# Dilated and windowed attention with expert adapters: masks and scores moved to all four 64x64 tiles of the TensorE array, row ends and last token chunks made full-array products

## The chip, the cores and the metric

The kernel runs on one core of a Trainium2 chip. The metric is device time in microseconds (us); lower is better. Engines are named as in the profile: PE is TensorE (matmul), PEld its weight loads, DVE is VectorE, ACT is ScalarE, POOL is GpSimd, SP issues some of the transfers. Matmul ends are modelled in the trace, so this text measures TensorE by the starts of its instructions wherever it can.

"Slow" is here a run over 1.5% above the fastest of the same kernel in its set. The kernel before had two groups of times on each of the three chips of the experiments, 119.3 to 120.8 us and 121.8 to 123.7 us. Comparisons below use fast runs. Chips also differ, by up to 2.2 us for the changed kernel, so kernels are compared within one call, which ran on one chip. Each mean is of two to four fast runs.

## The reference, cut to what matters

```python
# q, k, v: (8 batches, 8 heads, 576 positions, 64)
scores = q @ k.T / sqrt(64)
# heads 0-3: 0 <= rel < 32;   heads 4-7: 0 <= rel < 128 and rel % 4 == 0
attn = softmax(where(mask, scores, -1e9))
x = (attn @ v) as (8*576 tokens, 512)
logits = x @ w_gate                      # 8 experts, two chosen
out = x + sum over chosen e of w_e * (x @ A[e]) @ B[e]     # rank 16
```

## The kernel before

Positions of the dilated heads are reordered by residue, so every mask is a band. A score unit handles two heads of one batch ("hp" 0 to 3, so four units a batch). The 576 keys make nine blocks of 64; each block needs the scores of at most 96 queries. The masks are written to PSUM first, as a product with an identity, and the scores are added on top.

```python
def scores(b, hp):
    t = kqt(b, hp)                       # head a on partitions 64a .. 64a+63
    for k in range(2):                   # two PSUM banks: key blocks 0-4 and 5-8
        rows = slice(64 * k, 64 * k + 64)
        ...
        nc.tensor.matmul(banks[k][:, 0 : n * SEG], lhsT=two[rows], rhs=mask, start=True, ...)   # 64 x 128 tile
    for j in range(NB):
        k, c = divmod(j, 5)
        for a in range(2):
            rows = slice(64 * a, 64 * a + 64)
            nc.tensor.matmul(banks[k][rows, SEG * c : SEG * c + n],                               # 64 x 64 tile
                lhsT=t[rows, 0, 64 * j : 64 * j + 64], rhs=t[rows, 1, 64 * j : 64 * j + n], ...)
```

Only two of the four 64x64 tiles are used, the two that lie straight: head 0 goes from partitions 0-63 to 0-63, head 1 from 64-127 to 64-127.

Then follow the exponential (ACT, line 309), the products with the values (PE, lines 329 and 340), the division by the row sum (DVE, 351 and 352), a cast (POOL, 363), transposes (PE, 371), the gates (PE, 403), the routing (DVE, 424 to 444), the weighting (POOL, 449), transposes of the weighted hidden values (PE, 462), the expert outputs (PE, 486 and 498) and the final sums (DVE, 508 and 515). 576 tokens are four chunks of 128 and one of 64; the chunk of 64 takes part-array products:

```python
# end of the rows, in values():  64 columns of P: a 128 x 64 tile per head
nc.tensor.matmul(o[64 * h : 64 * h + 64, 260:390]..., lhsT=p[:, at : at + 64], rhs=bdv(b, hp, j), ...)
# gates():  m = 64 for the last chunk
nc.tensor.matmul(g[0:m, ...], lhsT=xt[:, k, 128 * c : 128 * c + m], rhs=AW[:, k], ...)
# gturn():  m = 64 for the last chunk
nc.tensor.transpose(tp[:, 128 * c : 128 * c + m], gz[0:m, c], ident[0:m, 0:m])
```

A small list scheduler in the kernel fixes the order of every engine's instructions in advance, from planned costs ("S" 620 ns, and so on). Engines then run in that order.

The softmax here doesn't subtract the row's maximum and nothing guards it: scores larger than these inputs give would overflow.

## Time and profile before

| | |
|---|---|
| time, median of 2 runs | 123.06 us |
| time / span of the profiled run, of the lower group | 120.8 / 119.0 us |
| last load lands | 75.0 us |
| last scores unit starts / last values product starts | 88.0 / 95.1 us |
| PE share of the chain of waits | 60% |

The first fence has lines of the kernel before's page: busy time of each engine, then busy tenths and the granted TensorE clock in 40 slices of 3 us, then the chain that ended last by engine (the work followed back from the last instruction, at each step to what released it).

```profile
PE 92.2 (77%) x1496; PEld 69.2 (58%) x1496; DVE 75.2 (63%) x220; ACT 70.4 (59%) x155; POOL 59.4 (50%) x86
...
PE   0105979999999999999999989999999915910540
...
DVE  6870536346578748996967759877986880193360
...
PEclk9999999999999999999999999999999997695555
...
PE 60%; DMA 13%; DVE 8%; POOL 8%; issue 5%; POOLq 1%; ACT 1%; DVEq 0%; ACTq 0%
```

PE stands at 9 in nearly every slice from 21 to 95 us, and the chain runs on PE for 60% of the span. Utilization alone would not prove the limit; the chain says that the work that ended last was, for that long, waiting for PE alone.

The second fence is the kernel before's timeline of PE: start, duration, line, what, tile rows*columns, output shape, count.

```profile
62.50 0.37 PE L290 MATMUL bs<-cb 64*128 64x480 bf16 x2
62.80 0.56 PE L298 MATMUL bs<-slot 64*64 64x96 bf16 x18
63.29 0.37 PE L290 MATMUL bs<-cb 64*128 64x480 bf16 x2
63.59 0.56 PE L298 MATMUL bs<-slot 64*64 64x96 bf16 x18
64.08 0.37 PE L290 MATMUL bs<-cb 64*128 64x480 bf16 x2
64.39 0.56 PE L298 MATMUL bs<-slot 64*64 64x96 bf16 x18
64.88 0.64 PE L329 MATMUL bs<-slot,p 128*128 128x130 bf16 x8
```

Read the starts, not the durations (which include latency): 62.50, 63.29, 64.08 are units 0.79 us apart. From mask to score is 0.30 us although 480 columns stream in 0.20 at the full clock: the other 0.10 goes where the tile shape changes. It changes again at the end of every unit. The single starts inside a unit are below (not a view of the profile; read from the trace's records, in us).

```
63.290 63.293 | 63.593 63.597 | 63.660 63.663 | 63.704 63.708 | 63.746 63.749 | ... | 63.959 63.963 | next unit 64.083
 2 masks        9 pairs of scores, 0.041 to 0.044 apart (0.067 after the first); then 0.120 to the next mask
```

### The profile page before, as it was taken

What the parts mean: (1) busy time and instruction counts of PE and PEld (TensorE: products, weight loads), DVE (VectorE), ACT (ScalarE), POOL (GpSimd) and SP (SyncE); (2) the same over time, 40 slices, a digit from 0 to 9 for tenths busy, and PEclk for the clock granted to TensorE, in tenths of its full rate; (3) what the DMA queues carried; (4) which work ended last, traced back from release to release, by engine and by line L of the source; (5) the groups of instructions that cost most, each with busy time, mean ns of one, the idle gap of its engine ahead of it and who ended that gap; (6) DMA issues with size and microseconds to landing.
All of it is one profiled execution on the core that took longest, in us unless ns stands there. A gap on an engine that the chain in (4) does not pass through costs nothing.

```text
span 119.0 us, 3669 instructions
## 1 busy us (share of the span) xinstructions
PE 92.2 (77%) x1496; PEld 69.2 (58%) x1496; DVE 75.2 (63%) x220; ACT 70.4 (59%) x155; POOL 59.4 (50%) x86
## 2 busy tenths in 40 slices
PE   0105979999999999999999989999999915910540
PEld 0005747777677778867787768787768704700210
DVE  6870536346578748996967759877986880193360
ACT  7927445868666868657776786668478633300200
POOL 6805172661798299259933850546266415404400
PEclk9999999999999999999999999999999997695555
DMA  3999999999999999999999999998640053009054
GB/s 102 223 212 219 208 217 218 208 215 213 215 211 220 210 213 217 211 215 213 218 210 216 215 216 353 427 424 378 274 195 6 0 248 149 0 0 396 0 219 178
DMA packets 4864, 24.64 MB, mean 207 GB/s; under 512 B 752, under 2 KB 1136, under 8 KB 3952
## 3 DMA queue, kind: packets, MB, share of 16 engines
q0 software_dynamic: 2848, 14.23, 58.9%
q1 hardware_dynamic: 2000, 10.19, 21.1%
q8 instruction: 11, 0.18, 0.6%
q14 instruction: 5, 0.04, 0.1%
HBM read 29.21 MB, written 9.44 MB: 325 GB/s over the span
## 4 chain that ended last, share of the span: by engine, by line
PE 60%; DMA 13%; DVE 8%; POOL 8%; issue 5%; POOLq 1%; ACT 1%; DVEq 0%; ACTq 0%
PE bs L329 14%; DMA slot<-in_kv_dram 13%; PE bs L298 12%; PE bs L403 10%; PE bs L371 6%; PE bs L290 6%; PE bs L486 5%; DVE x L508 3%; POOL slot L232 3%; PE bs L462 2%; PE bs L340 2%; POOL gz L449 2%; DVE x L352 1%; POOLq L636 1%; POOL gn L472 1%
## 5 line engine op out<-in xcount | busy, mean ns | idle before, releaser
L363 POOL CAST xb<-x 128x512 bf16<-128x512 f32 (+1 forms) x32 | 21.3, 671 | 30.7 <-DVE sm L444 15.3
L309 ACT ACTIVATE p<-bs 128x480 bf16<-128x480 f32 x64 | 30.9, 538 | 9.0 <-PE bs L298 7.8
L329 PE MATMUL bs<-slot,p 128*128 128x130 bf16 x352 | 27.4, 224 | 1.0 <-ACT p L309 1.0
L352 DVE TENSOR_TENSOR x<-bs,rc 128x384 f32<-128x384 f32 x48 | 26.8, 557 | 1.6
L508 DVE TENSOR_TENSOR x<-x,bs 128x512 f32<-128x512 f32 x32 | 20.2, 682 | 11.6 <-PE bs L486 11.4
L329 PEld LDWEIGHTS <-p 128*128 128x128 bf16 x352 | 21.8, 98 | 2.7 <-ACT p L309 1.7
L351 DVE RECIPROCAL rc<-bs 128x6 f32<-128x6 f32 x48 | 9.2, 191 | 22.2 <-PE bs L329 21.1
L298 PE MATMUL bs<-slot 64*64 64x96 bf16 (+1 forms) x576 | 18.8, 208 | 5.6 <-DMA slot<-in_kq_dram 5.4
L298 PEld LDWEIGHTS <-slot 64*64 64x64 bf16 x576 | 14.7, 109 | 13.3 <-issue 6.8
L232 POOL DMA_DIRECT2D slot<-in_kv_dram x32 | 16.7, 532 | 7.3 <-DMA slot<-in_kq_dram 4.7
L371 PE MATMUL bs<-cb,xb 128*128 128x128 bf16 x144 | 13.3, 220 | 3.9 <-POOL xb L363 3.9
L290 PE MATMUL bs<-cb 64*128 64x480 bf16 (+1 forms) x64 | 12.8, 363 | 3.4 <-DMA cb<-in_cb_dram 3.4
L449 POOL TENSOR_TENSOR gz<-zs,sm 128x640 bf16<-128x640 f32 x8 | 10.2, 1274 | 9.7 <-DVE sm L444 9.6
L472 POOL COPY gn<-gd 128x576 bf16<-128x576 bf16 x8 | 11.8, 1475 | 4.8 <-ACT gd L467 4.8
L391 ACT COPY xt<-bs 128x512 bf16<-128x512 bf16 x16 | 9.4, 587 | 6.5 <-PE bs L371 6.2
L403 PE MATMUL bs<-aw,xt 128*128 128x136 bf16 (+1 forms) x160 | 13.1, 236 | 0.0
L371 PEld LDWEIGHTS <-xb 128*128 128x128 bf16 x144 | 8.6, 97 | 5.8 <-POOL xb L363 4.3
L381 ACT COPY xt<-bs 128x512 bf16<-128x512 bf16 x16 | 9.4, 591 | 4.2 <-PE bs L371 4.1
L403 PEld LDWEIGHTS <-xt 128*128 128x128 bf16 (+1 forms) x160 | 10.7, 106 | 1.5 <-issue 0.2
L413 ACT COPY zs<-bs 128x408 f32<-128x408 f32 (+1 forms) x16 | 6.9, 443 | 5.4 <-PE bs L403 3.8
L462 PE MATMUL bs<-cb,gz 128*128 128x128 bf16 (+1 forms) x40 | 4.7, 235 | 6.4 <-POOL gz L449 6.2
L467 ACT ACTIVATE gd<-bs 128x576 bf16<-128x576 bf16 x8 | 5.2, 653 | 5.2 <-PE bs L462 4.3
(36 smaller groups left out, 75.4 us busy)
## 6 DMA issues: line engine op xcount, KB each, us to landing
slot<-in_kv_dram POOLq DMA_DIRECT2D x30, 434.2 KB, 13.9
out_dram<-x SPq DMA_DIRECT2D x7, 1152.0 KB, 6.9
out_dram<-x SPq DMA_DIRECT2D x2, 512.0 KB, 2.6
slot<-in_kq_dram POOLq DMA_DIRECT2D x2, 288.0 KB, 8.7
slot<-in_kv_dram POOLq DMA_DIRECT2D x2, 146.2 KB, 8.5
x<-in_aw_dram SPq DMA_DIRECT2D x1, 272.0 KB, 2.8
x<-in_bt_dram SPq DMA_DIRECT2D x1, 256.0 KB, 7.9
cb<-in_cb_dram SPq DMA_DIRECT2D x1, 208.0 KB, 2.6
```

Source lines behind the costliest of these rows:

```text
L232: insts[name] = nc.gpsimd.dma_start(out=dst, in_=src)
L290: nc.tensor.matmul(banks[k][:, 0 : n * SEG], lhsT=two[rows], rhs=mask, start=True, stop=False, skip_group_check=True)
L298: nc.tensor.matmul(banks[k][rows, SEG * c : SEG * c + n], lhsT=t[rows, 0, 64 * j : 64 * j + 64], rhs=t[rows, 1, 64 * j : 64 * j + n], star ...
L309: nc.scalar.activation(buf(("P", b, hp), P)[:, 5 * k : 5 * k + n, 0:SEG], buf(("S", b, hp), BS, k)[:, 0 : n * SEG].rearrange("p (j c) -> p ...
L329: nc.tensor.matmul(o[:, 130 * r : 130 * r + 130].rearrange("p (a d) -> p a d", a=2), lhsT=p[:, at : at + 128], rhs=bdv(b, hp, j), start=(n ...
L352: nc.vector.tensor_tensor(X[b][:, st, 3 * k : 3 * k + 3].rearrange("p r (a d) -> p r a d", a=2), o[:, :, :, 0:D], rc.unsqueeze(3).to_broad ...
L363: nc.gpsimd.tensor_copy(buf(("xb", b, hp), XB)[:, 0:n], X[b][:, st, 4 * h : 4 * h + n])
L371: nc.tensor.transpose(tp[:, 128 * u : 128 * u + 128], xb[:, u], ident)
L403: nc.tensor.matmul(g[0:m, GW * n : GW * n + GW], lhsT=xt[:, k, 128 * c : 128 * c + m], rhs=AW[:, k], start=(k == 0), stop=(k == 3), skip_g ...
L449: nc.gpsimd.tensor_tensor(buf(("gz", b), GZ).rearrange("p c (e r) -> p c e r", e=E), buf(("zs", b), ZS)[:, :, 0:ER].rearrange("p c (e r) - ...
L472: nc.gpsimd.tensor_copy(buf(("g", b), GN).rearrange("p (i c) -> p c i", c=C), buf(("g", b), GD).rearrange("p (c i) -> p c i", c=C),)
L508: nc.vector.tensor_tensor(x, x, d.rearrange("p (u h c) -> p u h c", u=2, h=2), ALU.add)
```

## The change

The intent is to run masks and scores on all four 64x64 tiles, so that the tile shape does not change inside a unit and four products run abreast, and to turn the 64-token leftovers into full-array products, so that the shape does not change there either. For the second half of the key blocks (bank 1), head 0 is sent to partitions 64-127 and head 1 to 0-63. The Trainium skill, "PSUM — Partial Sum Buffer", section "PSUM bank collisions raise a hardware error", says that row tiles may not write one bank and the same partitions at once; with the swap each bank is filled by two row tiles on different partitions. The values of those blocks are swapped on the host side of the layout to match.

```diff
 def scores(b, hp):
             for k in range(2):
-                rows = slice(64 * k, 64 * k + 64)
-                nc.tensor.matmul(banks[k][:, 0 : n * SEG], lhsT=two[rows], rhs=mask, start=True, ...)
+                for a in range(2):
+                    rows = slice(64 * a, 64 * a + 64)
+                    to = slice(64 * (a ^ k), 64 * (a ^ k) + 64)
+                    nc.tensor.matmul(banks[k][to, 0:n], lhsT=ident[rows, rows], rhs=CB[rows, at : at + n], start=True, ...)
-            for j in range(NB):
+            jobs = [(j, j, 64 * j, min(SEG, S - 64 * j)) for j in range(NB)]
+            if hp % 2:
+                jobs.append((9, 7, 512, 32))          # scores again, for the row end as a full-array product
+            for seg, j, q, n in sorted(jobs, key=lambda x: x[0] % 5):      # alternates the banks
                 ...
-                        banks[k][rows, ...]
+                        banks[k][to, ...]
 def values(b, st, k):     # end of the rows
-                        o[64 * h : 64 * h + 64, 260:390]..., lhsT=p[:, at : at + 64]      # 2 per head
+                    o[:, 260:390]..., lhsT=p[:, at : at + 128]                            # 4 accumulated
 def gates(b, part):
-                m = min(128, S - 128 * c)
+                at = min(128 * c, S - 128)            # last chunk overlaps the one before
 def gturn(b):  same, gz[:, c] whole
 # removed: setting parts of PSUM to zero at the start (pinit)
 # constants in SBUF: 832 -> 2048 columns (208 -> 512 KB)
 # planned costs: scores 620 -> 600 with 140 for a change of tile shape; others to what a trace showed
```

The cuts leave out the scheduler's new "mode" and the tables of constants. The issue order is planned anew, so it differs too.

More of the change, by code (lines that the diff above doesn't have):

```diff
@@ L45, in constants, with __init__ @@
     eye = np.eye(128, dtype=np.float32)
-    two = np.tile(np.eye(64, dtype=np.float32), (2, 2))
-    plain = np.tile(band(()), (2, 1))
-    dil = np.zeros((128, 5 * SEG), np.float32)
-    for j in range(NB):
-        m = band([e - 64 * j for e in (I, 2 * I, 3 * I)])
-        r, c = (0, j) if j < 5 else (64, j - 5)
-        dil[r : r + 64, c * SEG : (c + 1) * SEG] = m
-    return np.concatenate([eye, two, plain, dil], 1).astype(ml_dtypes.bfloat16)
+    none = np.full((64, SEG), NEG, np.float32)
+    last = np.where(np.arange(SEG) < 64, band(()), NEG)
+    spill = np.concatenate([band(())[:, 64:], none[:, 32:]], 1)
+    plain = [band(())] * 8 + [last, spill]
+    dil = [band([e - 64 * j for e in (I, 2 * I, 3 * I)]) for j in range(8)] + [last, spill]
+    m = np.concatenate(plain + dil, 1)
+    return np.concatenate([eye, np.concatenate([m, m], 0)], 1).astype(ml_dtypes.bfloat16)
 class Op:
-    def __init__(self, name, eng, dur, deps, prio, emit, alloc=(), free=(), lat=120):
+    def __init__(self, name, eng, dur, deps, prio, emit, alloc=(), free=(), lat=120, mode=0):
+        self.mode = mode
         self.name, self.eng, self.dur, self.deps = name, eng, dur, deps
@@ L68, in __init__, with add @@
         self.held = {}
-    def add(self, name, eng, dur, deps, prio, emit, alloc=(), free=(), lat=120):
-        op = Op(name, eng, dur, deps, prio, emit, alloc, free, lat)
+    def add(self, name, eng, dur, deps, prio, emit, alloc=(), free=(), lat=120, mode=0):
+        op = Op(name, eng, dur, deps, prio, emit, alloc, free, lat, mode)
         assert name not in self.ops, name
@@ L81, in order @@
         clock = {}
+        mode = 0
         todo = list(self.ops.values())
@@ L95, in order @@
                 t = clock.get(o.eng, 0.0)
+                if o.eng == "PE" and o.mode != mode:
+                    t += 140
                 for d in o.deps:
@@ L116, in order @@
             clock[o.eng] = o.end
+            mode = o.mode if o.eng == "PE" else mode
             for pool, key, n in o.alloc:
@@ L155, in attn_adapters_kernel @@
     X = [one.tile([128, 2, NB, 128], FP, name=f"x{b}") for b in range(B)]
-    P = [one.tile([128, NB, PER], BF, name=f"p{i}") for i in range(NP)]
+    P = [one.tile([128, NB + 1, PER], BF, name=f"p{i}") for i in range(NP)]
     XB = [one.tile([128, 5, 128], BF, name=f"xb{i}") for i in range(4)]
@@ L164, in attn_adapters_kernel @@
     RC = [one.tile([128, 3, 2], FP, name=f"rc{i}") for i in range(4)]
-    CB = one.tile([128, 256 + 6 * SEG], BF, name="cb")
+    CB = one.tile([128, 128 + 20 * SEG], BF, name="cb")
     AW = one.tile([128, 4, GW], BF, name="aw")
@@ L170, in attn_adapters_kernel @@
     ident = CB[:, 0:128]
-    two = CB[:, 128:256]
-    mplain = CB[:, 256 : 256 + SEG]
-    mdil = CB[:, 256 + SEG : 256 + 6 * SEG]
     stage = X[B - 1].rearrange("p s n c -> p (s n c)")
@@ L200, in pzeros @@
         return emit
-    def pinit():
-        for t in BS:
-            nc.vector.memset(t[64:128, GW : 2 * GW], 0.0)
     def first(name, fn, dur, nbytes):
@@ L211, in first @@
         add(name, "HQ", nbytes / 430.0, [name + "_i"], -1, emit, lat=900)
-    first("cb", lambda: nc.sync.dma_start(out=CB, in_=cb), 0, 128 * 832 * 2)
+    first("cb", lambda: nc.sync.dma_start(out=CB, in_=cb), 0, 128 * 2048 * 2)
     first("awf", lambda: nc.sync.dma_start(out=awf, in_=aw), 0, 128 * 544 * 4)
@@ L262, in attn_adapters_kernel @@
         add(f"pz{i}", "DVE", 520, [], -4 + i, pzeros(i))
-    add("pinit", "DVE", 900, [], -5, pinit)
     def kqt(b, hp):
@@ L276, in bdv, with segs @@
         ap = [list(x) for x in base.ap]
-        return bass.AP(base.tensor, base.offset, [ap[0], [V1, 2], [1, 65]])
+        if j < 5:
+            return bass.AP(base.tensor, base.offset, [ap[0], [V1, 2], [1, 65]])
+        return bass.AP(base.tensor, base.offset + V1, [ap[0], [-V1, 2], [1, 65]])
+    def segs(hp, k):
+        return 4 if k and hp % 2 == 0 else 5
     def scores(b, hp):
@@ L283, in emit @@
             for k in range(2):
-                rows = slice(64 * k, 64 * k + 64)
-                n = 5 - k
-                if hp < 2:
-                    mask = mplain[rows].unsqueeze(1).to_broadcast([64, n, SEG])
-                else:
-                    mask = mdil[rows, 0 : n * SEG]
-                nc.tensor.matmul(
-                    banks[k][:, 0 : n * SEG], lhsT=two[rows], rhs=mask, start=True, stop=False, skip_group_check=True
-                )
-            for j in range(NB):
-                k, c = divmod(j, 5)
-                n = min(SEG, S - 64 * j)
+                n = segs(hp, k) * SEG
+                at = 128 + 10 * SEG * (hp // 2) + 5 * SEG * k
                 for a in range(2):
                     rows = slice(64 * a, 64 * a + 64)
+                    to = slice(64 * (a ^ k), 64 * (a ^ k) + 64)
                     nc.tensor.matmul(
-                        banks[k][rows, SEG * c : SEG * c + n],
+                        banks[k][to, 0:n], lhsT=ident[rows, rows], rhs=CB[rows, at : at + n],
+                        start=True, stop=False, skip_group_check=True,
+                    )
+            jobs = [(j, j, 64 * j, min(SEG, S - 64 * j)) for j in range(NB)]
+            if hp % 2:
+                jobs.append((9, 7, 512, 32))
+            for seg, j, q, n in sorted(jobs, key=lambda x: x[0] % 5):
+                k, c = divmod(seg, 5)
+                for a in range(2):
+                    rows = slice(64 * a, 64 * a + 64)
+                    to = slice(64 * (a ^ k), 64 * (a ^ k) + 64)
+                    nc.tensor.matmul(
+                        banks[k][to, SEG * c : SEG * c + n],
                         lhsT=t[rows, 0, 64 * j : 64 * j + 64],
-                        rhs=t[rows, 1, 64 * j : 64 * j + n],
+                        rhs=t[rows, 1, q : q + n],
                         start=False, stop=True, skip_group_check=True,
@@ L307, in emit @@
         def emit():
-            n = 5 - k
+            n = segs(hp, k)
             nc.scalar.activation(
@@ L335, in emit @@
                 return
-            for h in range(2):
-                hp = 2 * st + h
-                p = buf(("P", b, hp), P).rearrange("p j c -> p (j c)")
-                for n, (at, j) in enumerate([(8 * PER, 8), (7 * PER + 64, 7)]):
-                    nc.tensor.matmul(
-                        o[64 * h : 64 * h + 64, 260:390].rearrange("p (a d) -> p a d", a=2),
-                        lhsT=p[:, at : at + 64], rhs=bdv(b, hp, j),
-                        start=(n == 0), stop=(n == 1), skip_group_check=True,
-                    )
+            jobs = [(0, 8 * PER, 8), (0, 7 * PER + 64, 7), (1, 8 * PER - 64, 8), (1, 9 * PER - 64, 7)]
+            for n, (h, at, j) in enumerate(jobs):
+                p = buf(("P", b, 2 * st + h), P).rearrange("p j c -> p (j c)")
+                nc.tensor.matmul(
+                    o[:, 260:390].rearrange("p (a d) -> p a d", a=2),
+                    lhsT=p[:, at : at + 128], rhs=bdv(b, 2 * st + h, j),
+                    start=(n == 0), stop=(n == 3), skip_group_check=True,
+                )
         return emit
@@ L400, in emit @@
             for n, c in enumerate(range(3) if part == 0 else range(3, 5)):
-                m = min(128, S - 128 * c)
+                at = min(128 * c, S - 128)
                 for k in range(4):
                     nc.tensor.matmul(
-                        g[0:m, GW * n : GW * n + GW], lhsT=xt[:, k, 128 * c : 128 * c + m], rhs=AW[:, k],
+                        g[:, GW * n : GW * n + GW], lhsT=xt[:, k, at : at + 128], rhs=AW[:, k],
                         start=(k == 0), stop=(k == 3), skip_group_check=True,
@@ L460, in emit @@
             for c in range(5):
-                m = min(128, S - 128 * c)
-                nc.tensor.transpose(tp[:, 128 * c : 128 * c + m], gz[0:m, c], ident[0:m, 0:m])
+                at = min(128 * c, S - 128)
+                nc.tensor.transpose(tp[:, at : at + 128], gz[:, c], ident)
         return emit
@@ L534, in attn_adapters_kernel @@
             t = t0 + hp * T / 4
-            add(f"S{b}{hp}", "PE", 620, loaded(b, st, h, "k") + ["cb", "pinit"], t, scores(b, hp), alloc=[("s", ("S", b, hp), 2)], lat=200)
+            add(f"S{b}{hp}", "PE", 600, loaded(b, st, h, "k") + ["cb"], t, scores(b, hp), alloc=[("s", ("S", b, hp), 2)], lat=200, mode=1)
             add(f"E{b}{hp}0", "ACT", 580, [f"S{b}{hp}"], t, exps(b, hp, 0), alloc=[("p", ("P", b, hp), 1)], free=[("S", b, hp)], lat=150)
-            add(f"E{b}{hp}1", "ACT", 490, [f"S{b}{hp}", f"E{b}{hp}0"], t, exps(b, hp, 1), free=[("S", b, hp)], lat=150)
+            add(f"E{b}{hp}1", "ACT", 580 if h else 490, [f"S{b}{hp}", f"E{b}{hp}0"], t, exps(b, hp, 1), free=[("S", b, hp)], lat=150)
             if h == 0:
@@ L550, in attn_adapters_kernel @@
                 fr = [("P", b, 2 * st)] + ([("P", b, hp)] if k else [])
-                add(f"V{b}{st}{k}", "PE", (440, 440, 530)[k], deps, t + 1.5 + k / 10, values(b, st, k),
+                add(f"V{b}{st}{k}", "PE", (470, 470, 580)[k], deps, t + 1.5 + k / 10, values(b, st, k),
                     alloc=[("s", ("O", b, st, k), 1)], free=fr, lat=200)
@@ L562, in attn_adapters_kernel @@
         for part in range(2):
-            add(f"G{b}{part}", "PE", 780 if part == 0 else 500, [f"U{b}{hp}" for hp in range(4)] + ["aw"], t, gates(b, part),
+            add(f"G{b}{part}", "PE", 710 if part == 0 else 480, [f"U{b}{hp}" for hp in range(4)] + ["aw"], t, gates(b, part),
                 alloc=[("s", ("G", b, part), 1)], free=[("xt", b)], lat=200)
@@ L570, in attn_adapters_kernel @@
         add(f"W{b}", "DVE", 195, [f"H{b}"], t + 2, weigh(b))
-        add(f"Y{b}", "POOL", 1500, [f"W{b}"], t + 2.5, gated(b), alloc=[("gz", ("gz", b), 1)], free=[("zs", b)])
+        add(f"Y{b}", "POOL", 1280, [f"W{b}"], t + 2.5, gated(b), alloc=[("gz", ("gz", b), 1)], free=[("zs", b)])
         add(f"K{b}", "PE", 300, [f"Y{b}"], t + 4, gturn(b), alloc=[("s", ("GT", b), 1)], free=[("gz", b)], lat=200)
         add(f"J{b}", "ACT", 650, [f"K{b}"], t + 4, gcopy(b), alloc=[("g", ("g", b), 1)], free=[("GT", b)])
-        add(f"M{b}", "POOL", 680, [f"J{b}"], t + 4.5, gnat(b))
+        add(f"M{b}", "POOL", 1480, [f"J{b}"], t + 4.5, gnat(b))
         for n, (st, half) in enumerate([(1, 0), (1, 1), (0, 0), (0, 1)]):
@@ L578, in attn_adapters_kernel @@
             add(f"A{b}{st}{half}", "DVE", 700, [f"D{b}{st}{half}"], t + 5.2 + n / 2, total(b, st, half), free=[("D", b, st, half)])
-        add(f"DE{b}", "PE", 260, [f"J{b}", f"M{b}", "bt"], t + 7, delta_end(b), alloc=[("s", ("DE", b), 1)], free=[("g", b)], lat=200)
+        add(f"DE{b}", "PE", 260, [f"J{b}", f"M{b}", "bt"], t + 7, delta_end(b), alloc=[("s", ("DE", b), 1)], free=[("g", b)], lat=200, mode=2)
         add(f"AE{b}", "DVE", 430, [f"DE{b}"], t + 7.2, total_end(b), free=[("DE", b)])
@@ L605, in layouts @@
     v = np.concatenate([v, np.ones_like(v[..., :1])], -1)
-    v = v.transpose(0, 1, 3, 5, 2, 4, 6).reshape(B, 2, 2, 64, VW)
+    v = v.transpose(0, 1, 3, 5, 2, 4, 6)
+    v = np.concatenate([v[..., :5, :], v[:, :, ::-1, :, :, 5:]], 5).reshape(B, 2, 2, 64, VW)
     kv = np.concatenate(
```

## The prediction

> **What bounds the kernel.** TensorE. The DMA's issues land one load (434 KB) every 2.08 us, 8.3 us a batch; the last lands at 75.0 us. The timeline shows the gate products of successive batches 11.3 to 12.1 us apart, so TensorE falls behind the loads. In the chain of waits TensorE leads almost unbroken from about 25 us (before, it waits for loads) to 95 us, with PE at 9 tenths in nearly every slice. From 95 us to 119 us the chain is latency of the last two batches (DVE, POOL, stores). Busy work per batch is about 8.5 us on DVE and 7.8 on ACT, set-up left out: close behind.
>
> **What the change removes,** from single instruction starts in the trace:
> - One scores unit (mask, then scores) takes 0.79 us from mask start to the next operation. Mask to first score is 0.30 us, of which streaming 480 columns is 0.20: about 0.10 is the switch from 64x128 to 64x64 tiles. The nine score pairs start 40 ns apart (96 columns at the full clock), 0.37 us in all; leaving costs 0.12. The Trainium skill, "TensorEngine Tiling (Array Packing)", Key Properties, says that changing the tiling mode drains TensorE and that tiles run in parallel; the trace agrees: 57 ns start to start within full-array products, 150 ns where the tile changes (about 0.095 lost), and products on two row tiles or two column tiles start 3 to 7 ns apart.
> - After: four mask products abreast (0.20), no switch, then five steps of four abreast (about 0.22), then one switch (0.10): 0.52 to 0.55 us, or about 0.44 where another scores unit follows. Saved: 0.25 a unit, somewhat more where units are neighbours, so 1.0 to 1.2 us a batch.
> - Gates: the last chunk is no longer a column tile: two switches and a slow first product, 0.22 us a batch. Gate transposes: up to 0.2. Row ends: about nothing before scores, 0.1 before a full-array operation.
> - Sum: about 1.5 us a batch of TensorE, from 11.4 to about 9.9. The setting of PSUM to zero goes too, off the path.
>
> **What it adds.** Constants grow from 208 to 512 KB ahead of the first loads: about 0.7 to 1 us later start (estimate from a load's 209 GB/s). The second exponential of every second unit has 480 columns for 384: 577 for 498 ns, 0.16 us of ACT a batch, not on the path.
>
> **How much is critical.** Some 70 us, 6.1 batch periods, are TensorE-bound. All of 1.5 us a period would give 9.3 us. I expect 80 to 90% of it, since DVE (8.5 of 9.9) and ACT (8.0) then leave little slack and the products wait for evictions more often; less 0.8 us at the start; the end's 24 us stay. Net 7.5 us: 115.5 us, range 112 to 119. Chances: faster by over 2% 0.90, within 2% 0.08, slower 0.02.
>
> **What would show each step.** Mask to first score 0.21 to 0.23 us; score groups of four within about 12 ns, groups 40 apart; a unit 0.45 to 0.55 us; gate products all 57 ns apart; gates 10 us apart from batch to batch; PE busy about 80 us; first scores about 0.8 us later; last load still at 75 to 76 us; the stretch from the last scores to the end unchanged.
>
> **What would make it wrong.** Two tiles on the same rows sharing their moving stream or weight loads: the unit stays near 0.7 us and the gain falls to 2 or 3 us. Or DVE or the round trip through ACT and POOL taking over, with TensorE gaps that eat the saving. Or the issue order, which is planned anew with the changed costs, delaying the last batches.

## The result, and the profile after

The changed kernel took 113.47 us (two runs, 113.27 and 113.68) against 123.06 us. The ratio is 0.922, with a 95% interval of 0.915 to 0.929. (Ratios are the mean time of one kernel's fast runs over that of the other's of the same rounds, so not quite the ratio of the medians.) Both timed runs of the kernel before lay in its upper group. On another chip, with three of the changed kernel's runs fast and four of the kernel before's, the means were 111.81 and 120.25 us: 8.4 us. On a third chip they were 114.01 and 119.97: 6.0 us. Fast runs against fast runs, the gain is thus 5 to 7%; the 7.8% of the first pair is against the upper group. (The profile of the kernel before, 120.8 us, is from the lower group, so the profiles may be set side by side.)

The first fence has the changed kernel's page lines; slices are 2.8 us.

```profile
PE 84.3 (75%) x1592; PEld 70.3 (63%) x1592; DVE 73.4 (66%) x212; ACT 70.4 (63%) x155; POOL 59.1 (53%) x86
...
PE   0227799898999759998999799999988716942530
...
DVE  6773315546869924699899389998898770671450
...
PEclk9999999999999985999999999999999995578555
...
DMA 33%; PE 22%; DVE 18%; ACT 9%; issue 7%; POOL 4%; POOLq 1%; DVEq 0%; ACTq 0%
```

The two slices at 8 and 5 in the clock's line, from 39 to 45 us, are looked at below. PE lost 8 us of busy time, and its share of the chain fell from 60% to 22%. Loads, DVE and ACT have the larger shares now. The next fence is the changed kernel's PE timeline over two neighbouring units.

```profile
81.29 0.39 PE L289 MATMUL bs<-cb 64*64 64x480 bf16 x4
81.49 0.33 PE L301 MATMUL bs<-slot 64*64 64x96 bf16 x14
81.64 0.37 PE L289 MATMUL bs<-cb 64*64 64x480 bf16 x2
81.65 0.25 PE L301 MATMUL bs<-slot 64*64 64x96 bf16 x4
81.73 0.36 PE L289 MATMUL bs<-cb 64*64 64x480 bf16 x2
81.85 0.46 PE L301 MATMUL bs<-slot 64*64 64x96 bf16 x20
82.38 0.39 PE L373 MATMUL bs<-cb,xb 128*128 128x128 bf16 x4
```

From mask to first score is now 0.20 us, pure streaming. Two units take 81.29 to 82.38, 1.09 us with the switch at their end, against 1.59 us for a pair before. The masks of the second unit start at 81.64 and 81.73, while scores of the first still run: tiles that are done with one unit go on to the next.

The gates show the other half of the change. The fence has pieces of the chain of waits in order of time (start, duration): the first line from the kernel before, where a batch's 20 gate products held the chain for 1.41 us.

```profile
48.14 1.41 PE bs L403 x20
```

In the changed kernel:

```profile
57.17 1.18 PE bs L405 x20
```

That is 0.23 us less for the same 20 products, most of it the two changes of tile shape that are gone (0.093 us each).

The next fence shows how the changed kernel waits. The first two lines are its PE timeline; in brackets, how long PE had been idle and what ended it.

```profile
38.40 0.20 PE L301 MATMUL bs<-slot 64*64 64x96 bf16 x1
40.44 0.40 PE L301 MATMUL bs<-slot 64*64 64x96 bf16 x17 [1.84 <-DMA slot<-in_kv_dram]
```

Up to here PE keeps up with the loads. The chain in the changed kernel rests on one load, from its issue at 24.46 to its landing at 40.39 us, while the transfers ran back to back. Its share of the chain (DMA 33%) overstates the waiting: PE was busy for 13.5 of these 15.9 us. In the kernel before, PE was already behind from about 25 us. The next lines are busy time in two stretches of the changed kernel: length, then PE, PEld, DVE, ACT, POOL (number of instructions), granted clock, DMA share, GB/s.

```profile
41.30:44.70 3.40, 3.40 (x50) 2.87 (x48) 1.50 (x4) 2.19 (x5) 2.03 (x4) 0.50 1.00 207
65.00:84.00 19.00, 18.37 (x388) 16.27 (x386) 17.39 (x53) 14.41 (x35) 10.12 (x13) 1.00 1.02 339
```

The first stretch comes just after the wait: the granted clock is halved for 3.4 us. In the second, DVE is busy 17.4 of 19 us. The kernel before, in the same stretch:

```profile
65.00:84.00 19.00, 18.51 (x319) 14.49 (x317) 13.96 (x39) 13.25 (x31) 9.72 (x11) 1.00 0.98 328
```

DVE was at 14.0 there. Over the whole stretch from 24 to 88 us, first the kernel before and then the changed one:

```profile
24.00:88.00 64.00, 63.23 (x1119) 48.45 (x1116) 47.89 (x145) 44.94 (x106) 36.93 (x51) 1.00 1.00 254
24.00:88.00 64.00, 59.37 (x1255) 52.14 (x1241) 49.80 (x151) 49.62 (x116) 39.87 (x54) 0.97 1.01 255
```

PE was idle there for 0.8 us before and for 4.6 after. The wait list of the changed kernel has 2.5 us of it for loads:

```profile
PE bs L301 <- DMA slot<-in_kv_dram: 2.5, 3, 1.8
```

The end is as it was: from the last values product to the end of the span, 24.0 us before (95.06 to 119.02) and 23.3 us after (88.64 to 111.89).

### The profile page after: what moved, and what is told of

Same layout as the page of the kernel before. It is cut to its first block, busy times and chain, and to the rows that moved or that the text cites. A ratio compares the mean times of both kernels' runs of the same rounds, so it can differ in the third digit from the quotient of the medians.

```text
span 111.9 us, 3835 instructions
## 1 busy us (share of the span) xinstructions
PE 84.3 (75%) x1592; PEld 70.3 (63%) x1592; DVE 73.4 (66%) x212; ACT 70.4 (63%) x155; POOL 59.1 (53%) x86
## 4 chain that ended last, share of the span: by engine, by line
DMA 33%; PE 22%; DVE 18%; ACT 9%; issue 7%; POOL 4%; POOLq 1%; DVEq 0%; ACTq 0%
DMA slot<-in_kv_dram 27%; DMA slot<-in_kq_dram 6%; ACT p L312 5%; PE bs L405 5%; DVE x L510 5%; DVE x L354 5%; PE bs L332 5%; PE bs L488 4%; PE bs L373 3%; POOL gz L451 2%; POOL xb L365 2%; DVE rc L353 2%; PE bs L464 1%; DVE x L517 1%; POOLq L639 1%
## 5 line engine op out<-in xcount | busy, mean ns | idle before, releaser
L312 ACT ACTIVATE p<-bs 128x480 bf16<-128x480 f32 x64 | 32.2, 562 | 8.8 <-PE bs L301 8.7
L332 PE MATMUL bs<-slot,p 128*128 128x130 bf16 x352 | 28.9, 230 | 1.3 <-DMA slot<-in_kv_dram 0.9
L332 PEld LDWEIGHTS <-p 128*128 128x128 bf16 x352 | 23.3, 102 | 3.0 <-ACT p L312 1.9
L301 PE MATMUL bs<-slot 64*64 64x96 bf16 (+2 forms) x608 | 15.6, 212 | 5.7 <-DMA slot<-in_kq_dram 2.9
L301 PEld LDWEIGHTS <-slot 64*64 64x64 bf16 x608 | 13.5, 114 | 8.8 <-DMA slot<-in_kv_dram 4.1
L353 DVE RECIPROCAL rc<-bs 128x6 f32<-128x6 f32 x48 | 9.1, 190 | 15.0 <-PE bs L332 11.4
L289 PE MATMUL bs<-cb 64*64 64x480 bf16 (+1 forms) x128 | 14.6, 398 | 4.3 <-DMA cb<-in_cb_dram 4.1
L373 PEld LDWEIGHTS <-xb 128*128 128x128 bf16 x144 | 9.8, 103 | 6.7 <-POOL xb L365 5.7
L405 PE MATMUL bs<-aw,xt 128*128 128x136 bf16 x160 | 12.4, 235 | 0.0
L405 PEld LDWEIGHTS <-xt 128*128 128x128 bf16 x160 | 11.1, 104 | 0.4
L289 PEld LDWEIGHTS <-cb 64*64 64x64 bf16 x128 | 5.1, 109 | 6.4 <-DMA cb<-in_cb_dram 4.1
```

The costliest lines, as they stand in the source:

```text
L289: nc.tensor.matmul(banks[k][to, 0:n], lhsT=ident[rows, rows], rhs=CB[rows, at : at + n], start=True, stop=False, skip_group_check=True,)
L301: nc.tensor.matmul(banks[k][to, SEG * c : SEG * c + n], lhsT=t[rows, 0, 64 * j : 64 * j + 64], rhs=t[rows, 1, q : q + n], start=False, sto ...
L312: nc.scalar.activation(buf(("P", b, hp), P)[:, 5 * k : 5 * k + n, 0:SEG], buf(("S", b, hp), BS, k)[:, 0 : n * SEG].rearrange("p (j c) -> p ...
L332: nc.tensor.matmul(o[:, 130 * r : 130 * r + 130].rearrange("p (a d) -> p a d", a=2), lhsT=p[:, at : at + 128], rhs=bdv(b, hp, j), start=(n ...
L373: nc.tensor.transpose(tp[:, 128 * u : 128 * u + 128], xb[:, u], ident)
L405: nc.tensor.matmul(g[:, GW * n : GW * n + GW], lhsT=xt[:, k, at : at + 128], rhs=AW[:, k], start=(k == 0), stop=(k == 3), skip_group_check ...
```

## Experiments

Theory A: TensorE alone still sets the pace, so that every 0.1 us of TensorE a batch is worth 0.6 us of time. Theory B: the limit has moved, to loads up to about 40 us and to TensorE and DVE together after.

### Call 1: parts of the change undone

**after_again** is the changed kernel, unedited.

> The changed kernel itself, as a control for the others of this call. Expected 113.5 us, ratio to the kernel before 0.92. First load lands between 7.6 and 9.3 us: if it lands nearer 9.3, the earlier start seen in the changed kernel's first profile was chance and not part of the change.

Measured: 111.81 us (mean of three fast runs; one of 113.44 counts as slow), ratio 0.928, faster than expected. The profile is of the slow run. Its first load landed at 6.97 us, earlier still than the range expected, so the early start was there again.

**scores_bank_order.**

```diff
-            for seg, j, q, n in sorted(jobs, key=lambda x: x[0] % 5):
+            for seg, j, q, n in sorted(jobs):
```

> Changed kernel, same instructions and same issue order of units; only inside one scores unit the score products go bank by bank instead of alternating between the banks, so two tiles work at a time instead of four. Unit expected 0.18 us longer (ten steps of 0.04 us instead of five, less overlap effects), 0.7 us a batch. Theory 'TensorE alone sets the pace from 25 to 95 us': 4 to 4.5 us slower than the changed kernel, 118 us. Rival 'loads set the pace up to 40 us and DVE with ACT after 60 us, TensorE only between': 1 to 2.5 us slower, 114.5 to 116 us.

Measured: 112.20 us, 0.4 us over the control (the runs of the two overlap), and the edit did not do what I meant it to. Two neighbouring units took 1.09 us, as in the changed kernel:

```profile
80.58 0.39 PE L289 MATMUL bs<-cb 64*64 64x480 bf16 x4
80.81 0.40 PE L301 MATMUL bs<-slot 64*64 64x96 bf16 x18
81.02 0.39 PE L289 MATMUL bs<-cb 64*64 64x480 bf16 x4
81.23 0.41 PE L301 MATMUL bs<-slot 64*64 64x96 bf16 x20
81.67 0.22 PE L373 MATMUL bs<-cb,xb 128*128 128x128 bf16 x1
```

The starts inside the first unit form two interleaved series of pairs (from the trace's records): 80.810, 80.853, 80.899, 80.940, 80.982 and 80.862, 80.929, 80.975, 81.016. The program has all five pairs of bank 0 ahead of the four of bank 1. The records do not name the bank, but two of them show which series is which: the pair at 80.982 has the signal that ends bank 0, and the pair at 81.016 is of 64 columns, as only the last block, in bank 1, is. So the fifth pair of the program was the eighth to start. The products of idle tiles thus started ahead of earlier ones of busy tiles, and the order inside a unit was of no account. The run says nothing on what four abreast is worth. To keep the masks on four tiles and only the scores on two was not run: two row tiles would then write the same bank and partitions.

**masks_two_tiles.**

```diff
-                for a in range(2): ...            # 64x64 masks on four tiles
+                rows = slice(64 * k, 64 * k + 64)
+                nc.tensor.matmul(banks[k][:, 0:n], lhsT=two[rows], rhs=CB[rows, at : at + n], ...)   # 64x128
```

> Changed kernel with the mask products back in their old form, two 64x128 tiles, scores still on four 64x64 tiles: the switch inside each scores unit is back (about 0.10 us, and up to 0.2 where units are neighbours), 0.4 to 0.8 us a batch. Theory 'TensorE alone': 2.5 to 5 us slower, 116 to 118.5 us. Rival 'only the middle third is bound by TensorE': 0.7 to 2 us slower.

Measured: 113.46 us, 1.65 us over the control. A pair of units:

```profile
81.13 0.37 PE L288 MATMUL bs<-cb 64*128 64x480 bf16 x2
81.43 0.40 PE L300 MATMUL bs<-slot 64*64 64x96 bf16 x18
81.76 0.38 PE L288 MATMUL bs<-cb 64*128 64x480 bf16 x2
82.07 0.40 PE L300 MATMUL bs<-slot 64*64 64x96 bf16 x20
82.40 0.40 PE L372 MATMUL bs<-cb,xb 128*128 128x128 bf16 x4
```

It takes 1.27 us: the 0.30 from mask to score is back, and nothing of the second unit can start early. About 0.09 us a unit, 0.36 a batch. Theory A would make 2.2 us of that; B's range holds the 1.65, but at this size the two are hardly told apart.

**ends_tiled** puts row ends, gates and gate transposes back as in the kernel before (the reverse of the diff above for those three functions).

> Changed kernel with row ends, last gate chunk and last gate transpose back on part-array tiles: about 0.22 + 0.1 to 0.2 + 0.05 us a batch more TensorE time, 0.4 us. Theory 'TensorE alone': 2 to 3 us slower, 116 us. Rival: 0.3 to 1.2 us slower. The gate chunks should again show about 0.15 us start to start at the tile change.

Measured: 114.66 us, 2.85 us over the control. This is more than theory B's range, and as much as A expected. It is the part of the change with the smallest edit and, undone, the dearest of this call. I cannot say from these runs why 0.4 us a batch costs more here than in masks_two_tiles; one difference is that gates and gate transposes lie on the round trip through ACT, DVE and POOL, which the masks do not, but no run tests that. The start of the loads may be another: in the profiles the first load landed at 8.23 us here and at 6.97 in the control, whose profile is of a slow run.

### Call 2: which engine binds

The same two cuts were made in both kernels, in batches 0 to 5 only, so that the last two batches' latency at the end is untouched. One takes 1.1 us a batch from DVE, the other 0.86 from TensorE by plan (15 products at the measured 59 ns make 0.89); both leave out work on purpose. The second made the result wrong; the first stayed inside the tolerance.

```diff
 def total(b, st, half):                      # "less_dve"
+            if b < 6:
+                x, y = x[:, :, :, 0:64], y[:, :, :, 0:64]
             nc.vector.tensor_tensor(x, x, y, ALU.add)
 def gates(b, part):                          # "less_pe"
-                for k in range(4):
+                for k in (range(4) if b > 5 else [3]):
```

> Kernel before, but in batches 0 to 5 each final sum adds only half of its columns (result wrong on purpose): about 0.27 us less DVE time for each of four sums, 1.1 us a batch, nothing taken from the last two batches. If TensorE alone bounds the kernel before: within 0.7 us of it. If DVE were a limit there too: 3 us faster or more.

> Kernel before, but in batches 0 to 5 the gate products use one of the four blocks of the contraction (result wrong on purpose): 15 products of 57 ns less, 0.86 us of TensorE a batch. TensorE-bound: 3.5 to 5 us faster (0.86 times the four to six batches that end in the TensorE-bound stretch).

> Changed kernel with the same cut of DVE work, 1.1 us a batch in batches 0 to 5. Theory 'after the change the limit has moved: loads up to about 40 us, then TensorE, ACT and DVE by turns': 0.7 to 2.5 us faster. Theory 'still TensorE alone': under 0.5 us.

> Changed kernel with the same cut of TensorE work, 0.86 us a batch in batches 0 to 5. Theory 'the limit has moved': 0.5 to 2 us faster, clearly less than the same cut gives in the kernel before. Theory 'still TensorE alone': 3.5 to 5 us faster, as in the kernel before.

| kernel, fast runs | us | kernel before, same call |
|---|---|---|
| before_less_dve | 121.53 (four runs, 120.8 to 122.0) | 119.85 (its upper group: 122.3) |
| before_less_pe | 115.50 | 119.85 |
| after_less_dve | 113.20 | 119.85 |
| after_less_pe | 113.17 | 119.85 |

In the kernel before, the cut of TensorE gives 4.35 us (upper group against upper group, 117.4 against 122.3 us, 4.9) and the cut of DVE nothing that is clear (three of its runs lie near the upper group, 121.8 against 122.3 us): TensorE was the limit, as predicted. In the changed kernel neither cut gives a clear gain; 113.2 us lies among the changed kernel's own 111.8 to 114.0 us on the other chips. This call had no control of its own, so small gains are not excluded by the times. Theory B, too, had expected more: 0.7 us or more from the one, 0.5 or more from the other. The profiles are sharper, because the start of the loads can be matched. In after_less_pe the first load landed at 7.44 us and in the changed kernel's first profile at 7.60, both fast runs with one halved clock near 40 us, though on different chips. Counted from that landing, the last two batches' gates started after 78.10 and 87.78 us in both. A cut of 0.86 us of TensorE in each of six batches moved them by nothing, in one profile of each. Theory A falls for the changed kernel.

Where the cut went can be read from 24 to 88 us of after_less_pe, first busy time, then its longest entry in the list of waits:

```profile
24.00:88.00 64.00, 55.76 (x1157) 47.12 (x1151) 49.85 (x151) 49.28 (x116) 39.35 (x54) 0.97 1.01 255
PE bs L301 <- DMA slot<-in_kv_dram: 4.1, 3, 1.8
```

PE's idle time rose from 4.6 to 8.2 us: 1.6 us more for loads, the rest mostly for POOL's casts and copies and for DVE. One wait for a load, of 1.06 us, ends at 61.95 us. So the loads do not stop mattering at 40 us: the faster PE meets them again.

Here are busy times from 65 to 84 us, columns as above, first after_less_pe:

```profile
65.00:84.00 19.00, 17.17 (x356) 14.52 (x353) 17.40 (x53) 14.52 (x35) 10.23 (x13) 1.00 1.02 339
```

and after_less_dve:

```profile
65.00:84.00 19.00, 18.79 (x386) 17.08 (x384) 14.36 (x50) 13.69 (x34) 9.35 (x11) 0.95 1.02 336
```

With less TensorE work DVE stays at 17.4 of 19; with less DVE work it falls to 14.4 and PE stands at 18.8. The busy shares agree with each taking over when the other is cut, but loads come in here too. after_less_dve has a wait for a load just before this stretch:

```profile
62.58 0.40 PE L301 MATMUL bs<-slot 64*64 64x96 bf16 x17 [1.83 <-DMA slot<-in_kv_dram]
```

The clock was then halved from 63.6 to 67.0 us (0.95 in its line for 65 to 84 us). What the cut of DVE would have given without that wait and that clock is not separated.

### Call 3: both cuts, two tiles only, another order

**after_control** is the changed kernel again.

> The changed kernel again, as the control of this call: 111.5 to 113.5 us. In a profile that falls on a run with a halved clock near 40 us, TensorE will have waited about 2 us for a load just before; in one without, it will not.

Measured: 114.01 us, above the range expected. Its profile has a wait of 2.15 us for a load that ends at 41.4 us, and the clock halved from 41.3 to 44.7, as expected. The first load landed at 8.84 us: the same kernel has had 7.60, 6.97 and 8.84 in its three profiles, so the start alone differs between profiles by up to 1.9 us.

**after_less_both** has both cuts of call 2 (result wrong).

> Changed kernel with both cuts at once in batches 0 to 5 (1.1 us DVE and 0.86 us TensorE a batch; result wrong on purpose). Neither alone gave anything. Theory 'after about 40 us TensorE and DVE are near balance, and each takes over when the other is cut': 1.5 to 3 us faster than the control. Rival 'a round trip through several engines or the fixed issue order sets the pace, not any engine's work': under 0.7 us.

Measured: 111.97 us, 2.0 us under the control, with one of four runs slow at 115.06 and left out. In the profiles, both with the first load at 8.8 us, the last batch's gates start at 94.94 us against 96.31. Cutting both gives more than either was seen to give alone, on another chip, which is what theory B asked for. The rival in the expectation, that the fixed issue order sets the pace, is not ruled out with it: replanned, below, gains 1.5 us from the order alone. The gain is also less than the 4.35 us that TensorE alone gave in the kernel before: this kernel, too, waits for loads (1.21 us at 27 us, and 1.19 and 1.22 us near 40 us), and no cut of work of these two shortens a load.

**straight_tiles.**

```diff
-                    to = slice(64 * (a ^ k), 64 * (a ^ k) + 64)      # both in masks and in scores
+                    to = rows
 # and the values' swap for blocks 5-8 taken back
```

> Changed kernel with masks and scores all on the two tiles that lie straight (64x64 each, rows and columns the same half), values put back to match: no switch inside a unit, but two products at a time, so a unit needs 0.4 us of mask and 0.4 us of scores, with nothing to run beside them: 0.8 to 0.9 us a unit against 0.45 to 0.55, 1.3 to 1.5 us a batch. If four abreast is what the time came from: 5 us slower than the control or more, back to about 118 us. If the removed switches alone made the gain: within 2 us of the control.

Measured: 116.31 us, 2.3 us over the control, between the two expectations. A pair of units:

```profile
84.10 0.55 PE L287 MATMUL bs<-cb 64*64 64x480 bf16 x4
84.49 0.54 PE L299 MATMUL bs<-slot 64*64 64x96 bf16 x18
84.87 0.57 PE L287 MATMUL bs<-cb 64*64 64x480 bf16 x4
85.27 0.55 PE L299 MATMUL bs<-slot 64*64 64x96 bf16 x20
85.76 0.40 PE L371 MATMUL bs<-cb,xb 128*128 128x128 bf16 x4
```

It takes 1.66 us, so 0.83 a unit, slightly longer than in the kernel before with its switches (0.79). All of the saving in masks and scores, four abreast and no switch, is thus undone here, about 0.3 us a unit or 1.15 us a batch. Yet only 2.3 us of the 6.0 us gain on this chip went with it. Theory A, at six batches, would have it cost 7 us. The busy times show what took up most of it:

```profile
24.00:88.00 64.00, 63.23 (x1248) 54.95 (x1245) 48.79 (x150) 47.65 (x112) 39.28 (x55) 1.00 1.02 257
```

PE's idle time is down from 4.4 us in the control to 0.8. The control's halved clock is missing too; 3.4 us at half the clock are at most 1.7 us of work (an estimate from the two numbers). So the slower PE filled time that the faster one spent waiting. What else the gain rests on is the full-array ends (2.85 us when undone alone, on another chip) and the new issue order, which no run separates; parts undone one at a time need not add up.

**replanned** keeps every instruction and changes three numbers of the scheduler.

```diff
-                    t += 140                                  # change of tile shape
+                    t += 100
+        late = 0 if loads else 3500                           # first load 3.5 us later
-            add(f"S{b}{hp}", "PE", 600, ...)
+            add(f"S{b}{hp}", "PE", 450, ...)
```

> Changed kernel, same instructions, issue order planned anew with costs as the traces show them: a scores unit 450 for 600 ns, a tile switch 100 for 140 ns, loads 3.5 us later. Theory 'the fixed order leaves TensorE waiting for loads near 38 to 40 us, with the clock halved after, and bunches four scores units near 59 us': 1 to 3 us faster than the control, no wait over 1 us of TensorE between 25 and 80 us. Rival 'the order does not matter': within 0.7 us.

Measured: 112.51 us, 1.5 us under the control (0.987); each of its four runs was faster than every run of the control. That is below 2%. The first loads of the two profiles landed within 0.12 us of each other (8.72 and 8.84). Its profile has the line

```profile
PE 42%; DVE 24%; issue 8%; DMA 7%; ACT 6%; POOL 6%; POOLq 1%; SPq 1%; DVEq 0%; ACTq 0%
```

Loads have 7% of the chain, against 22% in the control's profile, and no wait of PE over 0.85 us is left between 25 and 80 us, nor a halved clock. The four units in a row near 50 us remain, so that part of the expectation was not met. Which of the three numbers did it was not tested.

## Why the prediction was right or wrong

The time was right: 113.47 us in a range of 112 to 119, ratio 0.922 against 0.939 from the point forecast. Point by point:

- **TensorE bounds the kernel before:** right, and tested. The cut of 0.86 us a batch gave 4.35 us, the cut of DVE none that is clear.
- **A unit of 0.52 to 0.55 us, 0.44 next to another:** right in kind. Neighbours took 0.54 each in the changed kernel and 0.475 in replanned (a pair 0.95), both with their final switch. The Trainium skill's statement that a change of tile shape drains the array ("TensorEngine Tiling (Array Packing)", "Key Properties") agrees with 0.30 against 0.20 us from mask to score.
- **Groups of four within 12 ns, 40 ns apart:** seen in some groups; more often the two banks' pairs drift apart, in keeping with scores_bank_order, where they ran independently.
- **Gates 0.22 us a batch:** right, 0.23. The products are 59 ns apart, not 57.
- **PE busy about 80 us:** 84.3.
- **From 11.4 to 9.9 us a batch:** the size was off. Between the gates of batches 1 and 5 the period fell from 11.53 us (36.57 to 82.70) to 10.41 (34.98 to 76.63): 1.1 us of the 1.5 saved.
- **"Some 70 us, 6.1 batch periods, are TensorE-bound":** this step failed for the changed kernel. The faster TensorE catches up with the loads and waits for them until 40.4 us; after that, cuts of its work alone gave nothing that is clear, and PE's idle time from 24 to 88 us grew from 0.8 to 4.6 us. The gain stops where TensorE meets the loads, and later DVE and what hangs on it. That DVE is the other limit after 65 us is argued from its 17.4 busy us of 19 and from the run with both cuts; no run isolates it.
- **DVE and ACT leave little slack:** right in direction for DVE (17.4 of 19 us busy from 65 to 84 us). ACT's part was not tested.
- **A start 0.8 us later, for the larger constants:** wrong, and the estimate did not follow from its own number (304 KB more at 209 GB/s are 1.45 us). The constants did land later (4.06 against 3.34 us), but the first load landed at 7.0 to 8.9 us in the eleven profiles of kernels with the large constants and at 8.9 to 9.3 in the three with the small ones. What moved it was not found. In the two profiles compared above it landed 1.7 us earlier (7.60 against 9.31), so part of their difference of 7.1 us may not come from TensorE's pace at all.
- **The end's 24 us stay:** right, 23.3.

That the total came out near was in part luck: less of the saving came through than assumed, but nothing was lost at the start, and the two timed runs of the kernel before lay in its upper group.

## What to carry to other kernels

Count the changes of tile shape in a TensorE-bound kernel, from the starts of its instructions: here each cost about 0.1 us, and taking back the full-array products made of a few 64-wide leftovers cost 2.85 us, going back to half the tiles in the main stage 2.3 us (on another chip). Before summing up a saving over the whole span, ask where the faster engine will meet the next limit: here the loads took a good part, and DVE probably from 65 us. After such a change, plan a fixed issue order again with the measured costs; here three numbers gave another 1.5 us, on one chip.

## What the Trainium skill lacked or had wrong

- "TensorEngine Tiling (Array Packing)", "Key Properties": it says that a mode switch drains but gives no cost. Here 0.093 to 0.10 us: 152 to 153 ns start to start where full-array gates meet a column tile, against 59 ns inside a run of them; 0.30 against 0.20 us from mask to score.
- "TensorE: Matmul & The Clock Gate", "Part 3: Packing small matmuls": it says that matmuls start and end in program order. In scores_bank_order two series of pairs ran interleaved (80.810 and 80.853 us of the one, 80.862 of the other, 80.899 of the one again) where the program has one series after the other. With the signal and the width read there, a tile of the same mode starts ahead of earlier products of a busy one.
- The same section: one line says that weight loads overlap running matmuls only on different rows; another, that a background weight buffer also allows it. The runs side with the second. In straight_tiles one 64x64 tile started a 96-column product with new weights most often every 41 to 46 ns, and full-array gates take 59 ns for 136 columns, which makes 42 ns for 96. So its weight loads seem hidden behind its own products.
- The same page, "HAM oscillation": it gives idle gaps over about 3.4 us as the danger. Between 22 and 85 us of the profiles, the clock was halved for 3.4 us, from within 1 us of the end of single gaps of 1.76 (after_again), 1.83 (after_less_dve), 1.84 (the changed kernel), 1.85 (after_less_pe) and 2.15 us (after_control), and of two of 1.19 and 1.22 us close together (after_less_both). It was not after gaps of 1.60 (scores_bank_order) and 1.64 us (ends_tiled). Eight such cases do not make a threshold.
